# An attention stage that keeps its softmax unnormalised, sums its rows with a column of ones, and places its PSUM tiles by hand

## The chip, the cores and the metric

The program runs on one core of a Trainium2 chip. A core has TensorE (PE), VectorE (DVE), ScalarE (ACT), GpSimd (POOL), and SyncE (SP), which issues most of the DMAs. The metric is the time of one execution on the device in microseconds (us). The runs before the change took 784.77, 784.86 and 785.48 us, with a median of 784.86.

## The reference

An attention layer feeds two dense layers. Only the attention part is changed; the dense part stays as it is.

```
q, k, v: [4, 8, 576, 64]; M_prev: [4, 8, 64, 64]; z_prev: [4, 8, 64]; beta: [8]; all float32
scores = q k^T / 8, causal;   a = exp(scores - max) / (sum + 1e-9);   local = a v
phi(x) = where(x > 0, x, exp(x) - 1) + 1
mem    = (phi(q) M_prev) / (phi(q) . z_prev + 1e-6)
g      = 1 / (1 + exp(-beta))
x      = (g mem + (1 - g) local), heads side by side          -> [2304, 512]
x      = (h - tanh(h)) w_out,  h = x w_in                     (width 2048)
out    = layernorm(h softmax(h)) w_out2,  h = x w_in2         (width 1024)
```

## The kernel before

The work runs as one pass over 16 **pairs** of heads (a batch has 8 heads, so 4 pairs); then the first dense layer (class `Moe1`), then the second. The 576 queries of a head are four blocks of 128 and a tail of 64; the tails of two pairs are handled together, in the odd pair. The steps of a pair p, with lines of the kernel before:

- `load_q`, `load_k`, `load_v`: DMAs on SP. q arrives with queries on the partitions and is transposed on PE (`q_tp`, ten 64-column transposes, L224) and copied by DVE (`q_t`, L251). From pair 2 on k arrives in 32-row pieces that DVE turns itself (`k_t`, L256).
- `s_r`, `s_l`: scores on PE (L326, L342). `s_max` (L356): DVE adds the mask, moves the block from PSUM to SBUF (tile P, or PL for the tails) and takes the row's minimum of the negated scores. `s_exp` (L383): ACT, exp in place, with the row sum through `accum_out`, which is an instruction of its own in the trace (ACTIVATION_READ_ACCUMULATOR).
- `s_eps`, `s_inv` (L395, L399): DVE turns the sums into reciprocals. `s_norm` (L410): POOL multiplies each block of probabilities by the reciprocal and by 1 - g.
- `a_t` (L224): PE transposes the probabilities block by block into T; `a_ev` (L449): ACT copies T to SBUF (pt). `a_pv` (L473): PE multiplies v (the weights, 128x64) by pt, up to 256 moving columns at a time, into X.
- `f_neg` (POOL, L270), `f_exp` (ACT, L273), `f_max` (DVE, L277): phi(q) = max(q + 1, exp(min(q, 0))). `m_mm` (L291): PE, phi(q) times M and z. The weights hold both heads of the pair on 128 rows, against a block-diagonal MZ of 130 columns, into R. `m_eps`, `m_inv`, `m_mul` (L299, L303, L309): DVE divides. `a_mem` (L224): PE transposes that result into X, where `a_pv` adds to it. `x_ev` (L500): DVE copies X out; `x_mv` (L510): SP moves it by DMA into xT, the input of the dense layer.

PSUM holds three rotating "homes" of two banks (tag S) for scores, transposes and R, and a fourth (tag X) for the output of a pair alone. Order is by hand: two tables (`PROLOGUE` up to pair 7, `PERIOD` for two pairs from there) list the steps; each engine runs its instructions in the order in which they are emitted. `split_x` (L701 on ACT, L703 on POOL) splits xT by chunk of 128 channels (one pair of each batch) into a high and a low part, in `room` slots and after the pairs. `heat` (L212) is matmuls without use that keep PE running at the start. The first dense layer works on blocks n of tokens: H (L735) is h, Y (L767) is y; block 0 and 1 need only the first two batches, and twelve matmuls of H for block 0 stand among the last `a_pv`.

Of the kernel before, what the change touches and what calls it, by code (L numbers as in the profile page):

```python
# [15 lines left out]
P = 128  # L16
# [20 lines left out]

class Attention:
# [16 lines left out]
    def __init__(self, ap, sp, ps, tc, q, k, v, M_prev, z_prev, beta, xT, ident, mz):  # L55
# [44 lines left out]
        w = self.HP * 2 * self.MW  # L100
        t = mz.tile([P, 2048], F32, tag="G", name="MZ", bufs=2)
        for i in range(2):
            nc.vector.memset(t[:, w * i : w * i + w], 0.0)
            self.MZ.append(t[:, w * i : w * i + w].rearrange("p (c w) -> p c w", c=self.HP))
        self.qs = []
        for i in range(2):
            t = sp.tile([P, NC, 2, D], F32, tag=f"nq{i}", name=f"nq{i}", bufs=1)
            nc.vector.memset(t[D:P, NC - 1], 0.0)
            self.qs.append(t)
        self.poff = [P * c * (c + 1) // 2 for c in range(NC)]  # L110
        for name in ("tp", "x", "QT", "KT", "St", "e", "n", "ret", "xm", "mx", "sm", "P", "pt"):
# [19 lines left out]
    def g_inv(self, p):  # L131
# [3 lines left out]
        nc.vector.tensor_scalar(og, g, -1.0, 1.0, ALU.mult, ALU.add)  # L135

    def g_cpy(self, p):
        nc, og, D = self.nc, self.og, self.D
        pairs = og.rearrange("p (a c j) -> p c a j", c=2, j=2)
        ogL = self.ogL.rearrange("p (a j) -> p a j", j=2)  # L140
        for c in range(2):
            rows = slice(c * D, (c + 1) * D)
            nc.gpsimd.tensor_copy(ogL[rows], pairs[rows, c])

    def load_m(self, p):
# [6 lines left out]
        for j in range(2):  # L152
            rows, w = slice(j * D, (j + 1) * D), j * self.MW
            nc.sync.dma_start(
                out=t[rows, :, w : w + D],
# [3 lines left out]
                out=t[rows, :, w + D : w + D + 1],  # L159
# [3 lines left out]
    def m_gate(self, p):  # L163
# [3 lines left out]
        m = self.MZ[b % 2].rearrange("p c (j w) -> p (c j) w", w=self.MW)[:, :, 0 : self.D]  # L167
        g = self.g.unsqueeze(2).broadcast_to([P, self.H, self.D])
        self.nc.gpsimd.tensor_tensor(m, m, g, ALU.mult)

    def _natural(self, t, src, p, tail):
# [3 lines left out]
        for j in range(2):  # L175
            self.eng.dma_start(
                out=t[:, 0 : NC - 1, j],
# [3 lines left out]
            out=t[tail : tail + D, NC - 1], in_=src[b, h0 : h0 + 2, full : self.S].rearrange("h p d -> p h d")  # L181
# [6 lines left out]
    def load_k(self, p):  # L188

        D, Q = self.D, self.D // 2  # L190
        G = self.S // Q
        b, h0 = divmod(2 * p, self.H)
        t = self.sp.tile([P, P * self.NC], F32, tag="nk", name=f"k{p}", bufs=2)
        if p < self.KPE:
            t = self.nat["k", p] = t.rearrange("p (c j d) -> p c j d", j=2, d=D)
            self.nc.vector.memset(t[D:P, self.NC - 1], 0.0)
            self._natural(t, self.k, p, 0)
            return
        t = self.nat["k", p] = t[:, 0 : G * Q].rearrange("p (g d) -> p g d", d=Q)
        for j in range(2):  # L200
            for i in range(2):
# [1139 lines left out]
```

## Time and profile before

| | |
|---|---|
| median of three runs | 784.86 us |
| the profiled execution's own time | 784.9 us |
| its span, first to last instruction | 783.1 us, so 1.8 us lie around it |
| busy: PE, DVE, ACT, POOL | 768.6, 567.4, 343.8, 368.0 us |
| TensorE clock granted | 1.000 of full speed in the mean, full in all slices |

Busy time is the union of an engine's instructions. Matmuls overlap in the array, so a busy PE is not PE at its peak: for what a group of matmuls costs, take the distance from its start to the next group's start. The attention pairs fill about the first 187 us; from there to the end PE is busy without a visible gap.

### The profile page before, as it was taken

To read this page: it belongs to the slowest core of one execution; us is meant where nothing else is said; L and a number is where in the kernel's file an instruction comes from. 1 tells how busy PE (TensorE), PEld (TensorE's weight loads), DVE (VectorE), ACT (ScalarE), POOL (GpSimd) and SP (SyncE) were. 2 spreads that over 40 slices of the span, in tenths; PEclk is the share of its full clock that TensorE was granted. 3 is DMA by queue.
4 is the path that set the end of the run, shared out by engine and by line. 5 is a ranking of instruction groups with operands and counts; after the bars stand their busy time and mean duration, and the time that the engine had idled before them with its cause. 6 is when DMAs were issued, how large, how long until landed. Compare 5 with 4: busy or idle time off the path is not lost.

```text
span 783.1 us, 14732 instructions
## 1 busy us (share of the span) xinstructions
PE 768.6 (98%) x5646; PEld 648.3 (83%) x5646; DVE 567.4 (72%) x1100; ACT 343.8 (44%) x662; POOL 368.0 (47%) x352
## 2 busy tenths in 40 slices
PE   8999999999999999999999999999999999999998
PEld 6777767787888888888989889898898888888887
DVE  5999899973487786786867866677877766656651
ACT  4789999995223333332433333322422333322331
POOL 4998889976034333433433333234533444334431
PEclk9999999999999999999999999999999999999999
DMA  6665656611012221221112111112101334334341
GB/s 140 127 139 112 147 117 151 157 49 39 0 54 62 74 73 46 71 71 63 55 55 81 54 54 55 54 54 81 54 28 51 118 123 153 124 107 125 116 135 54
DMA packets 108389, 67.03 MB, mean 86 GB/s; under 512 B 85408, under 2 KB 94368, under 8 KB 108320
## 3 DMA queue, kind: packets, MB, share of 16 engines
q1 hardware_dynamic: 107120, 65.81, 30.4%
q8 instruction: 44, 0.72, 0.4%
q10 hardware_dynamic: 1200, 0.30, 0.2%
q14 instruction: 25, 0.20, 0.1%
HBM read 48.25 MB, written 13.11 MB: 78 GB/s over the span
## 4 chain that ended last, share of the span: by engine, by line
PE 87%; DVE 5%; POOL 3%; issue 2%; DMA 1%; ACT 1%; SPq 0%; DVEq 0%; ACTq 0%; POOLq 0%
PE H L735 25%; PE Y L767 25%; PE H L961 13%; PE X L473 4%; PE S L326 3%; POOL P L410 2%; DVE P L356 2%; PE R L291 2%; PE T L224 1%; DVE e L277 1%; PE heat L212 1%; PE O1X L1055 1%; PE O16X L1055 1%; PE O15S L1055 1%; PE O14X L1055 1%
## 5 line engine op out<-in xcount | busy, mean ns | idle before, releaser
L767 PE MATMUL Y<-G,wo 128*128 128x512 f32 (+1 forms) x960 | 204.4, 368 | 0.1
L767 PEld LDWEIGHTS Y<-G,wo 128*128 128x128 f32 x960 | 174.8, 188 | 24.4 <-issue 1.6
L735 PE MATMUL H<-xh,wi 128*128 128x512 f32 (+1 forms) x640 | 151.4, 369 | 0.0
L915 POOL TENSOR_TENSOR raw<-raw,cva 128x512 f32<-128x512 f32 x48 | 63.1, 1314 | 176.1 <-DVE cva L913 162.4
L735 PEld LDWEIGHTS H<-xh,wi 128*128 128x128 f32 x640 | 117.2, 188 | 16.0 <-issue 0.4
L749 ACT ACTIVATE t<-H 128x1024 f32<-128x1024 f32 (+1 forms) x40 | 37.7, 942 | 140.9 <-PE H L735 138.5
L961 PE MATMUL H<-w2i,Ys 128*128 128x512 f32 x384 | 89.6, 389 | 0.0
L410 POOL TENSOR_SCALAR P<-P,sm,og 128x512 f32<-128x512 f32 (+3 forms) x124 | 78.9, 651 | 15.2 <-DVE sm L399 8.6
L735 PE MATMUL H<-xT,wi 128*128 128x512 f32 (+1 forms) x320 | 84.6, 368 | 0.0
L961 PEld LDWEIGHTS H<-w2i,Ys 128*128 128x128 f32 x384 | 72.0, 188 | 14.9
L781 DVE TENSOR_TENSOR yT<-Y,yT 128x512 f32<-128x512 f32 (+3 forms) x105 | 77.2, 788 | 1.4 <-PE Y L767 1.2
L751 ACT CAST G<-t 128x1024 fp32r<-128x1024 f32 (+1 forms) x40 | 38.6, 965 | 84.0 <-DVE t L750 84.0
L752 DVE TENSOR_TENSOR G<-t,G 128x1024 fp32r<-128x1024 f32 (+1 forms) x40 | 45.7, 1143 | 40.4 <-ACT G L751 40.4
L383 ACT ACTIVATE P<-P,mx 128x512 f32<-128x512 f32 (+3 forms) x128 | 70.5, 556 | 2.6 <-DVE mx L356 2.5
L750 DVE TENSOR_TENSOR t<-H,t 128x1024 f32<-128x1024 f32 (+1 forms) x40 | 44.6, 1114 | 34.7 <-ACT t L749 34.6
L978 ACT ACTIVATE e<-H,s 128x1024 f32<-128x1024 f32 x18 | 20.1, 1118 | 109.6 <-DVE s L972 109.6
L735 PEld LDWEIGHTS H<-xT,wi 128*128 128x128 f32 x320 | 58.8, 188 | 7.6
L1310 POOL TENSOR_TENSOR Ys<-yT,Ys 128x512 fp32r<-128x512 f32 x16 | 20.7, 1297 | 93.2 <-ACT Ys L1309 80.4
L356 DVE CUSTOM_DVE_ANT_0 P<-S,mask 128x512 f32<-128x512 f32 (+3 forms) x128 | 56.4, 481 | 5.2 <-PE S L326 4.9
L449 ACT COPY pt<-T 128x1024 f32<-128x1024 f32 (+2 forms) x64 | 51.2, 826 | 14.5 <-PE T L224 13.6
L473 PE MATMUL X<-pt,v 128*64 128x64 f32 (+3 forms) x832 | 51.2, 272 | 0.0
L473 PEld LDWEIGHTS X<-pt,v 128*64 128x64 f32 x832 | 39.1, 137 | 12.5 <-issue 7.3
(208 smaller groups left out, 1207.9 us busy)
## 6 DMA issues: line engine op xcount, KB each, us to landing
raw<-in_moe_w_in_dram SPq DMA_DIRECT2D x24, 512.0 KB, 3.7
raw<-in_moe_w_out_dram SPq DMA_DIRECT2D x16, 512.0 KB, 3.4
D<-rest SPq DMA_DIRECT2D x16, 512.0 KB, 2.6
rest<-D SPq DMA_DIRECT2D x64, 128.0 KB, 3.0
out_dram<-ob SPq DMA_DIRECT2D x17, 256.0 KB, 3.0
nq<-in_q_dram SPq DMA_DIRECT2D x32, 128.0 KB, 2.9
v<-in_v_dram SPq DMA_DIRECT2D x32, 128.0 KB, 2.9
raw<-in_moe_w_out_dram SPq DMA_DIRECT2D x32, 128.0 KB, 2.6
```

What stands on the lines that cost most here:

```text
L356: self.nc.vector.tensor_tensor_reduce(out=self._block(p, i), in0=s, in1=mask, scale=-0.125, scalar=3.0e38, op0=ALU.add, op1=ALU.min, accum ...
L383: self.nc.scalar.activation(t, t, AF.Exp, bias=self.mx[p][:, i : i + 1], scale=-1.0, accum_out=self.sm[p][:, i : i + 1],)
L410: eng.tensor_scalar(d, d, self.sm[p][:, i : i + 1], og, ALU.mult, ALU.mult)
L449: self.copy(pt, T)
L473: self.nc.tensor.matmul(self.X[j * D : (j + 1) * D, to, D * c : D * (c + n)], v[:, kb, j, :], pt[:, r, D * at : D * (at + n)], start=False ...
L735: nc.tensor.matmul(H[a:z, f], wi[:, wl, c, f * P + a : f * P + z], self.x[n][xl][:, c], start=(count[f] == 0), stop=(count[f] == 3 * KD - ...
L750: nc.vector.tensor_tensor(t, H, t, ALU.subtract)
L752: nc.vector.tensor_tensor(G[:, 1], t, G[:, 0].bitcast(F32), ALU.subtract)
L767: nc.tensor.matmul(Y[d][:, 0:NB], wo[:, wl, f, d * P : (d + 1) * P], G[:, gl, f], start=(i == 0), stop=(i == 3 * KF - 1),)
L781: nc.vector.tensor_tensor(y, src, y, ALU.add)
L915: self.eng.tensor_tensor(w, w, a, ALU.add)
L961: nc.tensor.matmul(H[:, nh * 512 : (nh + 1) * 512], Y[:, yl, c, :], w2i[:, wl, c, nh * 512 : (nh + 1) * 512], start=(k == 0), stop=(k == 3 ...
```

## The change

- **Probabilities.** `s_exp` no longer sums, and `s_eps`, `s_inv` and `s_norm` are gone. v gets a 65th column of ones, so that PV yields the row sum as its last column.
- **PV by query.** `a_pv` swaps the operands: weights are 64 queries of pt, the moving operand is v with its ones (65 columns). 800 matmuls of 65 columns take the place of 416 of 64 to 256. The result X has queries on the partitions; `x_eps`, `x_inv`, `x_mul` (DVE) scale it by (1 - g)/sum, `x_add` (POOL) adds the memory part, `x_tp` (PE) transposes the sum, `x_ev` (now on ACT) copies it, `x_mv` moves it. `a_mem` is gone.
- **Feature map.** phi(q) = max(q, 0) + exp(min(q, 0)): `f_r` and `f_neg` on POOL, `f_exp` on ACT, `f_add` on POOL; `f_max` on DVE is gone.
- **Memory product.** `m_mm` takes one head at a time: 64 rows of weights against 65 columns of M and z, so each matmul uses a quarter of the array. 288 matmuls of 65 columns take the place of 128 of 130 and 64 of 65.
- **q.** From pair 2 on q is loaded in 32-row pieces and turned by DVE, as k is; 14 of 16 `q_tp` are gone.
- **PSUM.** All four homes are shared; the order names the home after an `@`.
- **Order.** One table for all 16 pairs replaces the two; 25 instead of 41 `heat` matmuls; all of H for block 0 and 8 of 24 matmuls of H for block 1 (`h:0`, `h:1`) stand among the last pairs.

```diff
         if tag == "S":
-            i, bufs = self.n % (3 if self.third else 2), 1
-            tag, self.n = f"S{i}", self.n + 1
-            if i == 2:
+            tag = f"S{self.homes.pop(0) if self.homes else self.n % 2}"
+            self.n, bufs = self.n + 1, 1
+            if tag == "S2":
+                tag = "X"
+            elif tag == "S3":
                 pool = self.third
...
-            t = ap.tile([P, NC, 2, D], F32, tag=f"v{i}", name=f"v{i}", bufs=1)
+            t = ap.tile([P, NC, 2, D + 1], F32, tag=f"v{i}", name=f"v{i}", bufs=1)
+            nc.gpsimd.memset(t[:, :, :, D : D + 1], 1.0)
             nc.gpsimd.memset(t[0:D, NC - 1], 0.0)
             self.vs.append(t)
...
-    def load_q(self, p):
-        t = self.nat["q", p] = self.qs[p % 2]
-        self._natural(t, self.q, p, 0)
...
+    def _load(self, name, src, p, t):
+
 
         D, Q = self.D, self.D // 2
-        G = self.S // Q
+        if p < self.KPE:
+            t = self.nat[name, p] = t.rearrange("p (c j d) -> p c j d", j=2, d=D)
+            self.nc.vector.memset(t[D:P, self.NC - 1], 0.0)
+            self._natural(t, src, p, 0)
+            return
...
+        t = self.nat[name, p] = t[:, 0 : self.S].rearrange("p (g d) -> p g d", d=Q)
         for j in range(2):
             for i in range(2):
                 at = j * D + i * Q
                 self.eng.dma_start(
                     out=t[at : at + Q],
-                    in_=self.k[b, h0 + j, :, i * Q : i * Q + Q].rearrange("(g p) d -> p g d", p=Q),
+                    in_=src[b, h0 + j, :, i * Q : i * Q + Q].rearrange("(g p) d -> p g d", p=Q),
                 )
...
+    def load_q(self, p):
+        self._load("q", self.q, p, self._next(self.qs))
+
+    def load_k(self, p):
+        self._load("k", self.k, p, self.sp.tile([P, P * self.NC], F32, tag="nk", name=f"k{p}", bufs=2))
...
+    def f_r(self, p):
+
+
+        w = self.fw[p] = self.sp.tile([P, self.S], F32, tag="fw", name=f"fw{p}", bufs=2)
+        if self.eng is self.nc.scalar:
+            self.eng.activation(w, self.QT[p], AF.Relu)
+        else:
+            self.eng.tensor_scalar_max(w, self.QT[p], 0.0)
+
     def f_neg(self, p):
-        e = self.e[p] = self.sp.tile([P, self.S], F32, tag="fe", name=f"e{p}", bufs=3)
-        self.eng.tensor_scalar_min(e, self.QT[p], 0.0)
+        e = self.e[p] = self.sp.tile([P, self.S], F32, tag="fe", name=f"e{p}", bufs=4)
+        self.nc.gpsimd.tensor_scalar_min(e, self.QT[p], 0.0)
...
-    def f_max(self, p):
+    def f_add(self, p):
         e = self.e[p]
-        self.nc.vector.scalar_tensor_tensor(e, self.QT[p], 1.0, e, ALU.add, ALU.max)
-        self.scores -= 1
+        self.nc.gpsimd.tensor_tensor(e, e, self.fw.pop(p), ALU.add)
...
     def m_mm(self, p):
...
-        for i in range(self.NC):
-            at = min(P * i, self.S - P)
-            for j, n in ((0, 1), (1, 1)) if i == self.NC // 2 else ((0, 2),):
-                r, u = divmod(2 * i + j, self.NC)
+        for i in range(n + p % 2):
+            for j in range(2):
                 for h in range(2):
+                    rows, q = slice(j * D, (j + 1) * D), p - 1 + h if i == n else p
+                    at = self.full if i == n else P * i + D * h
                     self.nc.tensor.matmul(
-                        R[h * D : (h + 1) * D, r, W * u : W * (u + n)], f[:, at + h * D : at + h * D + D],
-                        self.MZ[b % 2][:, c, W * j : W * (j + n)], start=True, stop=True, skip_group_check=True,
+                        R[h * D : (h + 1) * D, j, W * i : W * (i + 1)], self.e[q][rows, at : at + D],
+                        self.MZ[b % 2][rows, q % self.HP], start=True, stop=True, skip_group_check=True,
                     )
-        self.ret[p] = R[:, :, 0 : W * self.NC].rearrange("p r (u w) -> p r u w", w=W)
...
+    def _times(self, p, tag, t, n):
+
+        w = 2 * n.shape[2] * self.D
+        x = self.ap.tile([P, P * self.NC], F32, tag=tag, name=f"{tag}{p}", bufs=2)[:, 0:w]
+        n = n.unsqueeze(3).broadcast_to([*n.shape, self.D])
+        self.nc.vector.tensor_tensor(
+            x.rearrange("p (u r d) -> p r u d", r=2, d=self.D), t[:, :, :, 0 : self.D], n, ALU.mult
+        )
+        return x
...
     def m_eps(self, p):
-        n = self.n[p] = self.ap.tile([P, 2, self.NC], F32, tag="fn", name=f"n{p}")
+        n = self.n["m", p] = self._n(p)
         self.nc.vector.tensor_scalar_add(n, self.ret[p][:, :, :, self.D], 1e-6)
...
     def m_mul(self, p):
-        D = self.D
-        x = self.xm[p] = self.ap.tile([P, self.NC, P], F32, tag="xm", name=f"xm{p}", bufs=2)
-        n = self.n.pop(p).unsqueeze(3).broadcast_to([P, 2, self.NC, D])
-        self.nc.vector.tensor_tensor(
-            x.rearrange("p c (j d) -> p (c j) d", j=2).rearrange("p (r u) d -> p r u d", r=2),
-            self.ret.pop(p)[:, :, :, 0:D], n, ALU.mult
+        self.xm["m", p] = self._times(p, "xm", self.ret.pop(p), self.n.pop(("m", p)))
+
+    def x_eps(self, p):
+        n = self.n["x", p] = self._n(p)
+        GI = self.GI[:, p % self.HP, :, 0 : n.shape[2]]
+        self.nc.vector.scalar_tensor_tensor(n, self._units(self.X[p], p)[:, :, :, self.D], 1e-9, GI, ALU.add, ALU.mult)
+
+    def x_inv(self, p):
+        n = self.n["x", p]
+        self.nc.vector.reciprocal(n, n)
+
+    def x_mul(self, p):
+        self.xm["x", p] = self._times(p, "xa", self._units(self.X.pop(p), p), self.n.pop(("x", p)))
+
+    def x_add(self, p):
+        x, m = self.xm["x", p], self.xm.pop(("m", p))
+        self.eng.tensor_tensor(x, x, m, ALU.add)
+
+    def x_tp(self, p):
+        x = self.xm.pop(("x", p))
+        T = self.tp["x", p] = self._home(f"XT{p}")
+        self._turn(T, [x[:, P * c : P * (c + 1)] for c in range(self.NC - 1 + p % 2)])
+
+    def x_ev(self, p):
+        n = self.NC - 1 + p % 2
+        x = self.x[p] = self._next(self.xs)[:, 0 : P * n]
+        self.copy(
+            x.rearrange("p (n r w) -> p r n w", r=2, w=self.D), self._order(self.tp.pop(("x", p)), n)
         )
...
-            accum_out=self.sm[p][:, i : i + 1],
...
-    def s_norm(self, p, i):
-        d = self.P[p, "b", i]
...
-        eng = self.nc.vector if p == self.NP - 1 and i % 2 else self.nc.gpsimd
-        eng.tensor_scalar(
-            d, d, self.sm[p][:, i : i + 1], og, ALU.mult, ALU.mult
-        )
...
     GROUPS = [
-        [(j, 0, c) for j in range(2) for c in range(4)],
-        [(j, kb, c) for j in range(2) for kb, c in ((1, 1), (1, 2), (1, 3), (3, 3))],
-        [(j, 2, c) for j in range(2) for c in (2, 3)],
+        [(j, kb, 3) for j in range(2) for kb in range(4)],
+        [(j, kb, 2) for j in range(2) for kb in range(3)],
+        [(j, kb, c) for c in (1, 0) for j in range(2) for kb in range(c + 1)],
     ]
-
-    def a_mem(self, p):
-
-        x = self.xm.pop(p)
-        self.X = self._home(f"X{p}", "X")
-        self._turn(self.X, [x[:, c] for c in range(self.NC)], keep=True)
...
-    PV = [
-        [(0, 0, 4, 0)],
-        [(1, 1, 3, 0), (3, 3, 1, 3)],
-        [(2, 2, 2, 0)],
-    ]
...
     def a_pv(self, p, i):
 
-        D = self.D
-        v = self.vs[p % 3]
+
+        D, W, n = self.D, self.MW, self.NC - 1
+        if p not in self.X:
+            self.X[p] = self._home(f"X{p}")
+        X = self.X[p]
         if i < 3:
             todo = [
-                (kb, j, self.pt[p, i], r, at + j * len(self.GROUPS[i]) // 2, n, r, c)
-                for kb, c, n, at in self.PV[i] for r in range(2) for j in range(2)
+                (self.pt[p, i], at, self.vt[p], kb, j, r, c)
+                for at, (j, kb, c) in enumerate(self.GROUPS[i]) for r in range(2)
             ]
         else:
             todo = [
-                (kb, j, self.pt[p - p % 2, 3 + j], p % 2, kb, 1, 1, self.NC - 1)
-                for kb in range(self.NC) for j in range(2)
+                (self.pt[p, 3 + j], kb, self.vt[p - 1 + r], kb, j, r, n)
+                for j in range(2) for kb in range(n + 1) for r in range(2)
             ]
-        for kb, j, pt, r, at, n, to, c in todo:
+        for pt, at, v, kb, j, r, c in todo:
             self.nc.tensor.matmul(
-                self.X[j * D : (j + 1) * D, to, D * c : D * (c + n)],
-                v[:, kb, j, :],
-                pt[:, r, D * at : D * (at + n)],
-                start=False, stop=False, skip_group_check=True,
+                X[r * D : (r + 1) * D, j, W * c : W * (c + 1)],
+                pt[:, r, D * at : D * (at + 1)],
+                v[:, kb, j],
+                start=kb == 0, stop=kb == c, skip_group_check=True,
             )
...
-    def x_ev(self, p):
-        x = self.x[p] = self.ap.tile([P, P * self.NC], F32, tag="x", name=f"x{p}", bufs=2)
-        self.copy(
-            x.rearrange("p (c r w) -> p r c w", r=2, w=self.D), self._order(self.X, self.NC)
-        )
...
+    ORDER = """
+        load_q:0:s load_k:0:a heat:0:-:17@1 k_tp:0:-@0 load_q:1:s q_tp:0:-@1 k_t:0:a load_k:1:s
...
+        f_add:14:- h:0:-@2 a_ev:14:a:2 a_ev:14:a:0 x_tp:12:-@3 x_ev:12:a s_exp:15:-:1 s_max:15:-:7
...
+        for op in self.ORDER.split():
+            op, _, homes = op.partition("@")
+            name, i, engine, *part = op.split(":")
+            self.ps.homes = [int(h) for h in homes]
+            part = [int(x) for x in part]
...
-        def filler():
-            rooms.finish()
-            for n in range(2):
-                H = ps.tile([P, m.KF, 512], F32, tag="S", name=f"H0_{n}", bufs=2)
-                yield from m.h_step(0, n, H, per=4)
-
-        fill = filler()
-        some = islice(fill, 11)
+        def filler(n):
+            H = ps.tile([P, m.KF, 512], F32, tag="S", name=f"H0_{n}")
```

On PE, in the middle of the pass: the memory product R of one pair, and PV (X) of another, before. Weights come behind the arrow with the moving tile; the sizes are those of the output.

```order
L326 MATMUL S_2_1987<-kT_1782,qT_1887 128x384 x2
L473 MATMUL X_1936<-pt_2_1893,v_113 64x128 x4
L291 MATMUL R_2008<-MZ,e_1747 64x130 x4
L291 MATMUL R_2008<-MZ,e_1747 64x65 x4
L291 MATMUL R_2008<-MZ,e_1747 64x130 x4
L473 MATMUL X_1936<-pt_3_1812,v_113 64x64
L473 MATMUL X_1936<-pt_4_1804,v_113 64x64
```

The same place after the change, for pairs of the same parity.

```order
L408 MATMUL S_1_2339<-kT_2156,qT_2192 128x128 x2
L241 MATMUL XT_2344<-ident,xa_2073 128x64 x10
L322 MATMUL R_2368<-MZ,e_1766 64x65 x16
L514 MATMUL X_2388<-v_111,pt_0_2358 64x65 x16
L514 MATMUL X_2388<-v_111,pt_2_2276 64x65 x12
L514 MATMUL X_2388<-v_111,pt_1_2305 64x65 x12
L514 MATMUL X_2388<-v_117,pt_3_2162 64x65
L514 MATMUL X_2388<-v_111,pt_3_2162 64x65
```

R is now 16 (odd pairs 20) matmuls of 65 columns, PV 40 (odd pairs 60) of 65, and the transpose XT of the finished output stands ahead of the next pair's work.

On ACT, at the end of the attention pass, before: the last copies of transposed probabilities (pt), and the first casts of `split_x` for block 3 of the tokens (xh_3647; its chunk c needs pair 12 + c).

```order
L449 COPY pt_3_3409<-T_3_3393 128x640
L701 CAST xh_3647<-xT_84 128x384 x2
L449 COPY pt_2_3465<-T_2_3452 128x512
L449 COPY pt_1_3516<-T_1_3469 128x1024
L449 COPY pt_0_3518<-T_0_3499 128x1024
L701 CAST xh_3388<-xT_84 128x512 x4
L701 CAST xh_3647<-xT_84 128x384
L749 ACTIVATE t_0_3589<-H_0_3523 128x1024
```

After: xs<-XT_3714 and xs<-XT_3779 are `x_ev` of pairs 14 and 15, xh_3852 is block 3.

```order
L493 COPY pt_0_3618<-T_0_3582 128x1024
L380 COPY xs<-XT_3600 128x2x5x64
L961 CAST wo_124<-raw 128x512
L380 COPY xs<-XT_3714 128x2x4x64
L737 CAST xh_2635<-xT_83 128x512
L737 CAST xh_3852<-xT_84 128x384 x3
L380 COPY xs<-XT_3779 128x2x5x64
L785 ACTIVATE t_0_3803<-H_0_3410 128x1024
L789 CAST G_0_3802<-t_0_3803 128x1024
```

Three casts of block 3 (chunks of pairs 12, 13, 14) now stand ahead of `x_ev` of pair 15; before, two stood ahead of the last pair's copies. POOL has the same: the three subtractions of block 3 stand ahead of `x_add` of pair 15 (xa_3711).

```order
L739 TENSOR_TENSOR xT_83<-xT_83,xh_2635 128x512
L739 TENSOR_TENSOR xT_84<-xT_84,xh_3852 128x384 x3
L370 TENSOR_TENSOR xa_3711<-xa_3711,xm_3762 128x640
L739 TENSOR_TENSOR xT_84<-xT_84,xh_3753 128x512 x4
L739 TENSOR_TENSOR xT_84<-xT_84,xh_3852 128x384
```

And PE between the transposes of pair 14 (XT_3714) and pair 15 (XT_3779):

```order
L241 MATMUL XT_3714<-ident,xa_3541 128x64 x8
L771 MATMUL H_0_3410<-xh_1830,wi_123 128x512 x4
L322 MATMUL R_3728<-MZ,e_3213 64x65 x16
L322 MATMUL R_3728<-MZ,e_3096 64x65
...
L771 MATMUL H_0_3410<-xT_83,wi_123 128x512 x4
L771 MATMUL H_1_3770<-xh_2635,wi_123 128x512 x8
L241 MATMUL XT_3779<-ident,xa_3711 128x64 x10
L771 MATMUL H_1_3770<-xT_83,wi_123 128x512 x4
L771 MATMUL H_1_3770<-xh_2635,wi_123 128x512 x8
```

Sixteen matmuls of H and the 20 of R (the last four are single rows, of which one is shown) stand between the two; the other 16 of H for block 1 come behind XT of pair 15.

## Rows read from the trace of the kernel before

**Rows 1.** Page, parts 1 and 2: busy us (share) xinstructions; clock in 40 slices.

```profile
PE 768.6 (98%) x5646; PEld 648.3 (83%) x5646; DVE 567.4 (72%) x1100; ACT 343.8 (44%) x662; POOL 368.0 (47%) x352
PEclk9999999999999999999999999999999999999999
```

**Rows 2.** First 180 us: busy PE, PEld, DVE, ACT, POOL; clock; DMA share; GB/s.

```profile
0.00:180.00 180.00, 169.05 (x2766) 131.22 (x2768) 157.46 (x497) 153.20 (x390) 150.29 (x194) 1.00 0.57 125
```

**Rows 3.** PE's timeline, 160 to 215 us: start, us, line, tile, shape, records.

```profile
166.54 0.66 PE L473 MATMUL X<-pt,v 128*64 128x128 f32 x8
167.03 1.29 PE L291 MATMUL R<-MZ,e 128*64 128x130 f32 x24
168.15 2.50 PE L473 MATMUL X<-pt,v 128*64 128x64 f32 x44
170.58 1.52 PE L224 MATMUL T<-ident,P 64*128 64x64 f32 x40
171.94 0.48 PE L224 MATMUL X<-ident,xm 64*128 64x64 f32 x10
172.34 0.66 PE L473 MATMUL X<-pt,v 128*64 128x128 f32 x8
172.93 0.83 PE L224 MATMUL T<-ident,PL 64*128 64x64 f32 x20
...
189.67 1.98 PE L735 MATMUL H<-xh,wi 128*128 128x512 f32 x8
...
195.11 11.04 PE L767 MATMUL Y<-G,wo 128*128 128x512 f32 x48
```

**Rows 4.** PE's timeline, 99 to 122 us: groups of short matmuls.

```profile
100.21 0.29 PE L342 MATMUL S_L<-kT,qT 64*64 64x64 f32 x8
...
105.80 0.40 PE L291 MATMUL R<-MZ,e 128*64 128x65 f32 x8
...
116.45 0.47 PE L224 MATMUL N11q<-ident,nq 64*128 64x64 f32 x10
116.85 1.34 PE L291 MATMUL R<-MZ,e 128*64 128x130 f32 x24
```

**Rows 5.** Who PE waited for up to 187 us: total, times, longest.

```profile
PE T L224 <- DVE mx L356: 3.1, 5, 0.8
PE S L326 <- DVE mx L356: 1.6, 5, 0.4
```

**Rows 6.** ACT's groups up to 195 us: busy us, mean ns.

```profile
L383 ACT ACTIVATION_READ_ACCUMULATOR P<-P,mx 128x1 f32 x128 | 24.6, 192 | 0.0
...
L701 ACT CAST xh<-xT 128x384 fp32r<-128x384 f32 x8 | 3.7, 519 | 0.0
...
L251 ACT COPY kT<-N0k 128x640 f32<-128x640 f32 x1 | 0.7, 693 | 4.7 <-PE N0k L224 4.7
```

**Rows 7.** POOL's groups: busy us, mean ns.

```profile
L410 POOL TENSOR_SCALAR P<-P,sm,og 128x512 f32<-128x512 f32 (+3 forms) x124 | 78.9, 651 | 15.2 <-DVE sm L399 8.6 <-ACT pt L449 3.8 <-PE S L326 2.2
L270 POOL TENSOR_SCALAR e<-qT 128x576 f32<-128x576 f32 x16 | 29.1, 1818 | 5.4 <-DVE qT L251 5.3
...
L410 POOL TENSOR_SCALAR PL<-PL,sm,ogL 128x576 f32<-128x576 f32 x15 | 12.4, 826 | 2.0 <-ACT P L383 1.7
L915 POOL TENSOR_TENSOR raw<-raw,cva 128x512 f32<-128x512 f32 x4 | 5.2, 1299 | 0.0
```

**Rows 8.** DVE's groups up to 187 us: busy us, mean ns.

```profile
L277 DVE SCALAR_TENSOR_TENSOR e<-qT,e 128x576 f32<-128x576 f32 x16 | 18.3, 1146 | 0.0
L500 DVE COPY x<-X 128x640 f32<-128x640 f32 x16 | 13.1, 821 | 10.7 <-PE X L473 10.6
L309 DVE TENSOR_TENSOR xm<-R,n 128x640 f32<-128x640 f32 x16 | 13.0, 814 | 0.1
...
L395 DVE TENSOR_SCALAR sm<-sm 128x6 f32<-128x6 f32 (+2 forms) x32 | 9.7, 321 | 2.2 <-ACT P L383 2.2
```

**Rows 9.** DMA issues up to 185 us: times, KB each, median us to landing.

```profile
xT<-x SPq DMA_DIRECT2D x11, 256.0 KB, 2.4
```

More of the change, by code (lines that the diff above doesn't have):

```diff
@@ L23, in __init__ @@
     def __init__(self, pool):
-        self.pool, self.n, self.third = pool, 0, None
+        self.pool, self.n, self.homes = pool, 0, []
     def tile(self, shape, dtype, tag, name, bufs=1):
@@ L135, in g_inv @@
         nc.vector.tensor_scalar(og, g, -1.0, 1.0, ALU.mult, ALU.add)
+        nc.vector.reciprocal(og, og)
     def g_cpy(self, p):
[L138 to L143, printed above, removed]
+        D, GI, n = self.D, self.GI, self.NC - 1
+        g, og = (t.rearrange("p (c j) -> p c j", j=2) for t in (self.g, self.og))
+        for i in range(2):
+            rows = slice(i * D, (i + 1) * D)
+            self.eng.tensor_copy(self.gm[rows], g[rows, :, i])
+        for r in range(2):
+            self.eng.tensor_copy(GI[:, :, r, 0:n], og[:, :, r].unsqueeze(2).broadcast_to([P, self.HP, n]))
+        for i in range(2):
+            rows = slice(i * D, (i + 1) * D)
+            self.eng.tensor_copy(GI[rows, 1::2, :, n], og[rows, i::2])
     def load_m(self, p):
@@ L152, in load_m @@
         for j in range(2):
-            rows, w = slice(j * D, (j + 1) * D), j * self.MW
+            rows = slice(j * D, (j + 1) * D)
             nc.sync.dma_start(
-                out=t[rows, :, w : w + D],
+                out=t[rows, :, 0:D],
                 in_=self.M[b].rearrange("(c j) d e -> j d c e", j=2)[j],
@@ L158, in load_m @@
             nc.sync.dma_start(
-                out=t[rows, :, w + D : w + D + 1],
+                out=t[rows, :, D : D + 1],
                 in_=self.z[b].rearrange("(c j) (d o) -> j d c o", j=2, o=1)[j],
@@ new lines, in m_mm, with _n @@
+        if p % 2:
+            del self.e[p - 1], self.e[p]
+        self.ret[p] = self._units(R, p)
+        self.scores -= 1
+    def _n(self, p):
+        t = self.ap.tile([P, 2, self.NC], F32, tag="xn", name=f"n{p}", bufs=4)
+        return t[:, :, 0 : self.NC - 1 + p % 2]
+    def _times(self, p, tag, t, n):
[6 more added lines that the diff above has]
+        return x
@@ new lines, in x_ev, with x_mv @@
+    def x_ev(self, p):
[3 more added lines that the diff above has]
+            x.rearrange("p (n r w) -> p r n w", r=2, w=self.D), self._order(self.tp.pop(("x", p)), n)
+        )
+    def x_mv(self, p):
+        b, c = divmod(p, self.HP)
+        x, full, S = self.x.pop(p), self.full, self.S
+        for xt, t0, a, e in self.xT(b * S, b * S + full):
+            self.nc.sync.dma_start(out=xt[:, c, t0 : t0 + e].bitcast(F32), in_=x[:, a : a + e])
+        if p % 2:
+            tails = x[:, full:].rearrange("p (i w) -> p i w", i=2)
+            for xt, t0, a, e in self.xT(b * S + full, (b + 1) * S):
+                self.nc.sync.dma_start(
+                    out=xt[:, c - 1 : c + 1, t0 : t0 + e].bitcast(F32), in_=tails[:, :, a : a + e]
+                )
+        self.done.add(p)
@@ L333, in s_l @@
         nc, D, S, full = self.nc, self.D, self.S, self.full
-        t = [self.ps.tile([P, 1024], F32, tag="S", name=f"S{p}_L{j}", bufs=2) for j in range(2)]
+        t = [self.ps.tile([P, 1024], F32, tag="S", name=f"S{p}_L{j}") for j in range(2)]
         for j in range(2):
@@ L351, in s_max @@
         if p not in self.mx:
[L352 to L355 removed]
+            self.mx[p] = self.ap.tile([P, self.LAST + 2], F32, tag="mx", name=f"mx{p}")
         self.nc.vector.tensor_tensor_reduce(
@@ L612, in run @@
+    """
+    def run(self, fills):
+        nc = self.nc
         on = {
@@ L622, in emit @@
             getattr(self, name)(i, *part)
[L624 to L650 removed]
+        for op in self.ORDER.split():
[3 more added lines that the diff above has]
+            part = [int(x) for x in part]
+            if name == "room":
+                self.room(int(i), *part)
+            elif name == "h":
+                next(fills[int(i)], None)
+            else:
+                emit(name, int(i), engine, part)
+            yield
 class Moe1:
@@ L1158, in attention_moe_kernel @@
             drain.finish()
-            for _ in fill:
-                pass
+            for f in fills:
+                for _ in f:
+                    pass
     ps.third = None
```

330 lines of the change are left out of this document (154 added, 176 removed).

## The prediction

> **What bounds the kernel now.** I read the page first. PE is busy for 98% of the span and its clock is granted in full throughout [rows 1]; the reader is to see that no clock can be won or lost, and that in the dense layers, where nothing is changed, time is PE's alone. So what the attention stage gains or loses comes through in full. Next came the busy time of the first 180 us, which hold nearly all of the stage [rows 2]: PE 169.1, DVE 157.5, ACT 153.2, POOL 150.3. All four are 83 to 94% busy, so one engine made lighter would gain little by itself: the next would hold the stage.
>
> Then I read PE's timeline for what a group costs, from its start to the next one's [rows 3]. R (`m_mm`) takes 167.03 to 168.15, 1.12 us. PV of a pair is a group of 8 (0.49) and one of 44 (168.15 to 170.58, 2.43), 2.92 together. `a_mem` takes 0.40 (171.94 to 172.34), and so does a `q_tp` (116.45 to 116.85) [rows 4]. R comes once a pair: from 116.85 to 167.03 are five pairs, 10.0 us each [rows 3, 4]. PE's waits are short and mostly for DVE to free a PSUM home (`s_max`), 3.1 and 1.6 us in all [rows 5]. PE is therefore nearly closed up, and the forecast is made on PE, with a check that no other engine comes in its way.
>
> **The price of a 65-column matmul.** PV's, R's and S_L's matmuls use half or a quarter of the array, and several run at once. Two groups of 8 records give the price [rows 4]: R's last 8, on column halves, run two at a time, four positions, and take 0.40; S_L's last 8, on quarters, run four at a time, two positions, and take 0.29. With a latency l and a step s for each further position, l + 3s = 0.40 and l + s = 0.29, so s = 0.055 and l = 0.235. A position costs 0.055 us whether it holds two matmuls or four. Each matmul of the program is two records here (832 of PV for 416).
>
> **PE, part by part.**
> - PV: 800 matmuls, 50 a pair, 100 records on column halves, 50 positions: 2.75 us, against 2.92 now. The 65 columns may cost a little more than in R's few, so I take no change; the bound is -0.17 a pair, -2.7 in all.
> - R: 288 matmuls, 18 a pair, 36 records on quarters, 9 positions: 0.50 against 1.12. That is -0.62 a pair, -9.9 in all. If they ran only two at a time, 18 positions would cost 0.99, and the gain is 2.1 in all. I take the quarters, since S_L shows them.
> - `q_tp`: 14 fall away, 14 x 0.40 = -5.6.
> - `a_mem` of ten transposes becomes `x_tp` of nine on average: 16 x 0.04 = -0.6.
> - Fewer `heat` matmuls, at the start, where PE waits for data: nothing; what covers it is that wait, and without it the 16 matmuls would be a further gain.
> - Switches between ways of dividing the array: a group of 8 takes 0.49 when R, divided alike, follows, and 0.59 (172.34 to 172.93) when a transpose, divided otherwise, follows [rows 3]: 0.10 a switch. The Trainium skill, "TensorEngine Tiling (Array Packing)", Key Properties, says that changing the tiling mode, not just the tile, drains TensorE; the trace agrees. It speaks against this change, since R leaves the division that it shared with PV. Counted along PE's order up to the first Y there are 85 switches before and 90 after: +0.5. Without any price for them the sum would be 0.5 lower.
>
> Together -15.6. PE will not turn all of it into time, since it will reach some probabilities sooner than they are ready: I take nine tenths, -14.0.
>
> **The other engines, so that none takes PE's place.** ACT loses the sums, 24.6 us, and 16 of the same kind for the tails at 0.19 (3.1), and gains `x_ev` at 0.69 (the copy of 640 from PSUM) or less, at most 11.1 [rows 6]: 153.2 becomes 136.6. POOL loses `s_norm`, 78.9 + 12.4; it gains `f_r`, priced as `f_neg` at 29.1 in all, and two adds a pair of 576 elements on average; the nearest row has 1.30 for two inputs of 512, so 1.46 each, 46.8 in all [rows 7]: 150.3 becomes 134.9. DVE loses `f_max` (18.3), `x_ev` (13.1) and `s_eps` (9.7), and gains `x_mul` as `m_mul` (13.0) with `x_eps` and `x_inv` at no more than `s_eps` cost a piece (32 x 0.32 = 10.3) [rows 8]: 157.5 becomes at most 139.7; q's transposes take the place of copies of the same number. Each engine thus falls by some 15 to 18, as PE does, and the balance stays as it is. In place of an `s_norm` that held back transposes, POOL's `f_r`, `f_neg` and `f_add` now hold back R, and `x_add` the XT; both have a pair or more of other work ahead of them.
>
> **The end of the stage.** Here the order adds a wait. `x_tp` of pair 15 waits for `x_add`, and on POOL this stands behind three subtractions of block 3, the last of which needs pair 14 in xT. From the end of XT of pair 14: `x_ev` 0.69, the DMA 2.4 [rows 9], a cast of 384 at 0.52 [rows 6], the subtraction 0.97 (1.30 for 512, by columns), `x_add` of 640 at 1.62 (by columns) [rows 7]: 6.2. PE has 16 matmuls of H at 0.227 (24 records from 189.67 to 195.11 [rows 3]), 3.6, R at 0.55 for pair 15 and four switches: 4.6. It waits for the other 1.6, and behind XT stand the rest of H and all of Y. On ACT, `x_ev` of pair 15 stands behind the same chunk's cast, and the tanh of H behind it. I take +2; bounds 0 (the DMA lands early) and 6.2 (nothing covers it).
>
> **Sum.** -14.0 + 2 = -12. The profiled execution took 784.9 us (span 783.1 and 1.8 around it), as the median of the runs, 784.86: 773.
>
> **Rivals.**
> - *R does not run four at a time.* For: the quarters of S_L belong to one group of 64 columns, and R changes weights with every matmul. Against: so does S_L. Cost 7.8 of the gain: 780. By the Trainium skill, "TensorE: Matmul & The Clock Gate", section "Wait — 56ns, not 53.3ns?", start-to-start never drops below about 25 ns: R's 576 records would then take 14.4 us in place of 8.0, and the time would be 779. The rows of S_L disagree: 8 records within 0.055 and a latency.
> - *The waits go too.* Four shared homes and a lighter DVE take away PE's 4.7 us of waits for `s_max` [rows 5], all of the -15.6 arrives, and the end costs nothing: 784.9 - 15.6 - 4.7 = 764.6.
> - *The gain stays in the waits.* PE reaches each probability sooner, but the chain scores, exp, transpose, copy keeps its length, and the pairs follow one another every 10.0 us as before: 784 to 786, no change.
> - *Slower: `x_ev` on ACT.* It stands in ACT's order among exps and copies, which wait behind it, and PE behind these. It needs `x_add` on POOL, behind `f_neg` and `f_r` at 1.8 each. For: ACT is in the cycle now. Against: the order puts `x_ev` a pair or more behind its PV. If it is late by 0.75 us a pair, the gain is gone; at 1.0 us, 16 us more: 789.
>
> **Chances and range.** The forecast 0.57 (its own range 768 to 778), R in twos 0.10, the waits go 0.20, no change 0.07, slower 0.06. The range takes in the second and third with their bounds and leaves the last two out: 764 to 782. A change of 0.2% is 1.6 us, about what a measurement of this kernel can tell from none: faster 0.87, same 0.07, slower 0.06.
>
> **What would show it.** In the profile after: R's group of 32 or 40 records takes about 0.5 us to the next start; PV's 80 to 120 records some 55 ns a position; R follows R every 9.1 to 9.3 us; POOL, ACT and DVE each lose 15 us or more up to the end of the stage; PE waits 1 to 3 us ahead of XT of pair 15; Y starts 11 to 14 us earlier than at 195.1. The prediction is wrong if R is paced in twos, if PE's waits for POOL or ACT grow by more than 0.3 us a pair, or if the dense layers change in length.

## The result, and the profile after

The changed kernel takes 778.5 us (median of 8 runs, 775.0 to 782.5), the kernel before 785.2 in the same rounds: a ratio of 0.9915, 95% interval 0.9888 to 0.9941. It is faster by just under one per cent, and the time lies within the range, but of the 12.1 us that were forecast 6.7 arrived. The profiled execution is the best of the eight: 775.0, span 773.2, so 9.9 under its counterpart of before.

Windows after, to be held against [rows 2] (columns as there), the second ending where Y starts:

```profile
0.00:180.00 180.00, 165.27 (x3622) 133.75 (x3624) 126.51 (x444) 148.42 (x263) 127.28 (x111) 1.00 0.62 127
0.00:184.71 184.71, 169.44 (x3642) 136.86 (x3642) 127.76 (x446) 151.14 (x267) 127.28 (x111) 1.00 0.61 125
```

The same window of before, up to its first Y:

```profile
0.00:195.11 195.11, 184.16 (x2870) 142.73 (x2871) 161.10 (x500) 160.73 (x403) 160.00 (x203) 1.00 0.53 118
```

Y starts 10.4 us earlier; what follows takes 588.5 in place of 588.0. So the whole difference lies in the attention stage. PE's busy time up to Y fell by 14.7, and its idle time rose from 10.9 to 15.3. PE's timeline after shows both (start, us, then as in [rows 3]; what PE waited for in brackets):

```profile
98.64 0.81 PE L322 MATMUL R<-MZ,e 64*64 64x65 f32 x40
99.38 2.55 PE L514 MATMUL X<-v,pt 128*64 128x65 f32 x80
104.01 0.53 PE L241 MATMUL T<-ident,PL 64*128 64x64 f32 x10 [2.08 <-DVE mx L435]
105.09 0.92 PE L408 MATMUL S<-kT,qT 64*128 64x384 f32 x4 [0.56 <-DVE n L359]
...
110.31 0.69 PE L322 MATMUL R<-MZ,e 64*64 64x65 f32 x32
110.93 3.14 PE L514 MATMUL X<-v,pt 128*64 128x65 f32 x100
115.63 0.80 PE L514 MATMUL X<-v,pt 128*64 128x65 f32 x20 [1.56 <-issue]
...
160.66 2.55 PE L514 MATMUL X<-v,pt 128*64 128x65 f32 x80
163.15 0.53 PE L241 MATMUL T<-ident,PL 64*128 64x64 f32 x10
...
168.18 3.72 PE L514 MATMUL X<-v,pt 128*64 128x65 f32 x120
171.83 0.46 PE L241 MATMUL XT<-ident,xa 64*128 64x64 f32 x8
...
175.14 2.01 PE L771 MATMUL H<-xh,wi 128*128 128x512 f32 x8
179.80 0.53 PE L241 MATMUL XT<-ident,xa 64*128 64x64 f32 x10 [2.65 <-POOL xa L370]
```

R takes 0.74 (98.64 to 99.38) or 0.62, on average 0.68 where [rows 3] had 1.12. PV takes 2.49 or 3.65, on average 3.07 against 2.92. And PE stands still at three places that [rows 5] do not have: 2.08 at 102, 1.56 at 114 and 2.65 at 177. The last was forecast. The second has no cause that the profile names ("issue": PE waited for nothing that it shows), and it is not k's: end_mz, a run below in which k is in time, has it at the same matmuls (its timeline):

```profile
111.69 0.81 PE L514 MATMUL X<-v,pt 128*64 128x65 f32 x21 [1.59 <-issue]
```

The first begins at a wait that the kernel before had nowhere, DVE's for k (the waits, 20 to 185 us: total, times, longest):

```profile
DVE kT L274 <- DMA k<-in_k_dram: 11.7, 7, 3.9
```

DVE stops in its order at the transpose of k (3.9 us, up to 100.7), and the masked scores behind it, which PE needs out of their PSUM homes, come late. SP, which issues that k, shows why (SP's timeline; here the time is that of issuing):

```profile
93.73 2.16 SPq L209 DMA_DIRECT2D nq<-in_q_dram  x4
95.94 3.01 SPq L209 DMA_DIRECT2D k<-in_k_dram  x4
99.05 2.47 SPq L388 DMA_DIRECT2D xT<-xs  x4
```

Each row starts where the one ahead ended. From 49.6 to 146.0 the rows of SP add up to 91.5 of 96.4 us, short waits within a row counted in; in the kernel before, the same stretch adds up to 79.7, with four gaps of 2 to 4 us. q now takes four issues a pair in place of three, and the pairs come faster.

### The profile page after: what moved, and what is told of

Its sections match the earlier page's. It is cut to its first block, busy times and chain, and to the rows that moved or that the text cites. A ratio compares the mean times of both kernels' runs of the same rounds, so it can differ in the third digit from the quotient of the medians.

```text
span 773.2 us, 16000 instructions
## 1 busy us (share of the span) xinstructions
PE 754.5 (98%) x6418; PEld 642.4 (83%) x6418; DVE 535.3 (69%) x1046; ACT 338.0 (44%) x534; POOL 344.7 (45%) x268
## 4 chain that ended last, share of the span: by engine, by line
PE 86%; ACT 4%; DMA 3%; DVE 3%; SPq 2%; POOL 1%; issue 1%; DVEq 0%; ACTq 0%; POOLq 0%
PE Y L806 25%; PE H L771 25%; PE H L1000 13%; PE X L514 4%; PE S L408 3%; PE T L241 2%; DMA k<-in_k_dram 1%; SPq L209 1%; ACT pt L493 1%; DVE P L435 1%; PE S_L L424 1%; PE R L322 1%; ACT P L462 1%; DMA xT<-xs 1%; PE O1X L1094 1%
## 5 line engine op out<-in xcount | busy, mean ns | idle before, releaser
L462 ACT ACTIVATE P<-P,mx 128x512 f32<-128x512 f32 (+3 forms) x128 | 67.0, 564 | 0.6 <-DVE mx L435 0.6
L493 ACT COPY pt<-T 128x768 f32<-128x768 f32 (+2 forms) x64 | 51.0, 827 | 9.6 <-PE T L241 9.4
L514 PE MATMUL X<-v,pt 128*64 128x65 f32 x1600 | 51.2, 223 | 2.2 <-issue 2.1
L514 PEld LDWEIGHTS X<-v,pt 128*64 128x64 f32 x1600 | 48.4, 138 | 4.7 <-issue 3.2
L408 PE MATMUL S<-kT,qT 64*128 64x256 f32 (+3 forms) x256 | 44.1, 454 | 2.0 <-DVE n L359 1.7
```

The lines of the kernel that those rows point to most:

```text
L408: nc.tensor.matmul(s, Q[rows, P * r : P * r + P], K[rows, 0:w], start=True, stop=True, skip_group_check=True,)
L462: self.nc.scalar.activation(t, t, AF.Exp, bias=self.mx[p][:, i : i + 1], scale=-1.0,)
L493: self.copy(pt, T)
L514: self.nc.tensor.matmul(X[r * D : (r + 1) * D, j, W * c : W * (c + 1)], pt[:, r, D * at : D * (at + 1)], v[:, kb, j], start=kb == 0, stop= ...
```

## Where the other half went: a control

The profiled execution was at full clock; the listed runs were not. Their mean granted clock goes from 1.000 (775.0) down to 0.989 (782.5), while before's runs read 0.999 or 1.000.

**again** is the changed kernel unedited.

> The changed kernel once more, with nothing edited, as the measure of the three others. If the spread of its times (775.0 to 782.5) goes with the granted clock, as the listed means of 1.000 to 0.989 suggest, this run's profile may hold a stretch where the clock is under full, and the windows show where. Expected 775 to 782 by both theories.

It took 779.6 (779.1 to 781.3). One of its windows, and under it the same one of the first profile, which had full clock:

```profile
140.00:160.00 20.00, 16.95 (x394) 13.35 (x392) 13.01 (x49) 16.30 (x31) 15.45 (x12) 0.91 0.47 130
```

```profile
140.00:160.00 20.00, 19.17 (x480) 15.74 (x477) 14.72 (x55) 19.45 (x37) 16.18 (x12) 1.00 0.47 133
```

A mean of 0.91 over 20 us is some 3.6 us at 1.2 in place of 2.4 GHz; from 100 to 120 us it is 0.91 as well, behind a wait of 1.95. PE's timeline of this run puts the one shown behind a wait too:

```profile
141.29 2.64 PE L514 MATMUL X<-v,pt 128*64 128x65 f32 x80
146.43 0.52 PE L241 MATMUL T<-ident,PL 64*128 64x64 f32 x10 [2.50 <-DVE mx L435]
147.51 1.15 PE L408 MATMUL S<-kT,qT 64*128 64x384 f32 x4 [0.56 <-DVE n L359]
...
149.23 2.20 PE L424 MATMUL S_L<-kT,qT 64*64 64x512 f32 x16
151.36 1.13 PE L241 MATMUL T<-ident,P 64*128 64x64 f32 x28
```

S_L's 16 records take 2.13 to the next start; in the first profile, which kept its clock, they take 1.14 there (146.36 to 147.50). The chain of waits names what came late: 

```profile
138.78 4.26 DMA k<-in_k_dram
```

At 62 us both executions are level. From there to Y again needs 3.9 us more:

```profile
62.10:188.70 126.60, 115.36 (x2618) 93.26 (x2616) 84.81 (x289) 105.32 (x185) 87.47 (x63) 0.97 0.54 120
```

```profile
62.00:184.71 122.71, 112.57 (x2618) 91.91 (x2616) 83.60 (x290) 105.03 (x185) 87.26 (x63) 1.00 0.55 123
```

2.8 of them are PE's busy time, the same matmuls at a mean clock of 0.97; 1.1 are idle time.

## The experiments

Two theories stood against each other. *SP's issues set the pace*: the loads are late because their queue never stops. *Slow transfers*: they are late because q's and k's 128-byte pieces take long (this k 4.3 us, the median 2.7). All times below are medians of 4 to 6 runs, next to before at 784.9 to 785.6.

**mv_act**: in `x_mv`, `nc.sync.dma_start` becomes `nc.scalar.dma_start`.

> Only x_mv (the transfers of the finished output into xT) is issued from ACT's queue in place of SP's. Theory 'queue': between 50 and 146 us SP issues without a gap, and k and v arrive late because of it (DVE waits 11.7 us for k); x_mv is 27 of SP's 134 us. Then k is no longer waited for, PE's idle time between 22 and 175 us (9.0) falls by 2 to 4, and the median falls by 2 to 5 us, or by less if ACT, which then issues, becomes late. Rival 'transfer': k is late because the 16 DMA engines are busy with 128-byte pieces (share 0.62); then the same bytes take as long from either queue, DVE's waits for k stay, and the time stays within 1 us or rises.

787.7, and DVE waited for k as long as in again (15.5 and 13.3). But SP got a wait of its own (SP's waits, 20 to 180 us):

```profile
SPq L209 <- DMA xT<-xs: 14.2, 5, 4.6
```

By its letter this is the rival's outcome (k is waited for as before, the time rises). But SP's loads stood waiting for transfers of the other queue, so SP was not freed, and the run tells nothing of either theory.

**mv_pool**: the same with `nc.gpsimd.dma_start`.

> x_mv issued by POOL in place of SP. From ACT's queue it made SP wait 14 us for the transfers into xT, so that run told nothing of the theories. If POOL's queue does not hold SP back, theory 'SP's issues set the pace' expects SP's stretch of 27 us to be free for loads, k in time and 772 to 777; the rival 'slow transfers' 778 or more. If POOL takes over 1 us for an issue, f_r, f_neg and f_add behind it come late and the time rises above 780 whatever the cause.

772.7 (768.9 to 776.5): 6.9 under again, as the theory of the issues expects. DVE's waits for k fall, of the same bytes in the same pieces:

```profile
DVE kT L274 <- DMA k<-in_k_dram: 3.5, 3, 1.8
```

**more_issues** and **fewer_issues** change the number of issues and hardly anything else; the second leaves out part of the loads, as its expectation says.

```diff
-        self.eng.dma_start(
-            out=t[tail : tail + D, NC - 1, :, 0:D], in_=src[b, h0 : h0 + 2, full : self.S].rearrange("h p d -> p h d")
-        )
+        for j in range(2):
+            self.eng.dma_start(out=t[tail : tail + D, NC - 1, j, 0:D], in_=src[b, h0 + j, full : self.S])
```

> The tail of v in two transfers in place of one: one more issue on SP a pair, the same bytes in the same pieces. Theory 'SP's issues set the pace': SP issues back to back between 50 and 146 us at 0.5 to 0.6 us each, so some ten more of them put every load behind by up to 6 us; k and v come later, PE waits more, the time rises by 2 to 6 us against the changed kernel (779). Rival 'the transfers themselves are slow' (the k that is waited for takes 4.3 us to land): an issue more of a small transfer changes nothing, 779 within 1.5.

> Left out: the loads of v's last 64 rows from pair 4 on and of z from the third batch on (what stands there already is used in their place), 16 of SP's issues, some 10 us of its time, and under 3% of the bytes. Theory 'SP's issues set the pace': k and v are in time, DVE's waits for k (12 to 13 us) halve at least, PE's waits of about 2 us behind them go, and with them the clock's two drops of 3.4 us; 772 to 776. Rival 'slow transfers': k is waited for as before, 778 to 780.

788.0 and 772.3: 8.4 over and 7.3 under again. DVE's waits for k, first with more, then with fewer:

```profile
DVE kT L273 <- DMA k<-in_k_dram: 16.1, 5, 8.2
```

```profile
DVE kT L276 <- DMA k<-in_k_dram: 4.9, 4, 2.8
```

The second is as the theory expects: sixteen issues fewer give 7.3. The first goes beyond its 2 to 6, and its trace says less for the theory than its time does. The line that it changes also loads q and k of the first two pairs, so 20 issues are added, four of them at the start. Up to Y the profiled execution is 8.9 behind again's, and 5.9 of these are there at R of pair 1 (in again at 41.85):

```profile
22.70 1.24 PE L321 MATMUL R<-MZ,e 64*64 64x65 f32 x32 [1.80 <-POOL MZ L180]
...
47.73 0.81 PE L321 MATMUL R<-MZ,e 64*64 64x65 f32 x40
```

There R waits for M, and the clock is at its lower level from 23 to 36 us. So it is the runs that take issues off SP that show what SP costs. That a slow transfer adds to a single wait (4.3 us in again) is not excluded; it is not what decides.

**end_dve**: `x_add:15:p` becomes `x_add:15:v`, `x_ev:15:a` becomes `x_ev:15:v`. **mz**: in `load_m`, the four `nc.sync.dma_start` of a batch become `nc.gpsimd.dma_start`. **end_mz**: both.

> x_add and x_ev of pair 15 on DVE in place of POOL and ACT, so that neither stands behind the subtraction and the cast of block 3. The step 'end of the stage' of the prediction: PE's wait of 2.65 us ahead of XT of pair 15 goes, Y starts 2 to 3 us earlier, and the time falls by 2 to 3 us. Rival: something else ends last there (the transfer of pair 14 into xT, the casts of H); then the wait reappears behind XT and the time stays within 0.7 us.

> The changed kernel with only the loads of M and z issued by POOL; pair 15 as in the change. With end_dve and end_mz it completes a square of two edits: 779.6 with neither, 776.4 with the end's edit, 766.6 with both. If the two are independent: 769 to 771, with the wait of 2 to 3 us ahead of XT of pair 15 still there and the clock whole up to there. Rival: the gain of end_mz over end_dve needed the end's edit (its wait too lets the clock fall); then 772 to 776.

> As end_dve (x_add and x_ev of pair 15 on DVE), and the loads of M and z issued by POOL, 16 issues less on SP with nothing left out. Theory 'SP's issues set the pace': 1 to 4 us under end_dve's 776.4, most of it around 100 us, where four such issues (2.6 us) stand ahead of the k that is waited for. Rival: within 1 us of end_dve.

776.4, 770.1 and 766.6, against 779.6 with neither: -3.2, -9.5 and -13.0, so the two add up; for end_mz only 1 to 4 under end_dve had been expected. mz leaves nothing out and moves the same bytes. Its waits for k, and the loads of k in again and in mz (60 to 180 us: issues, KB each, median us to landing):

```profile
DVE kT L274 <- DMA k<-in_k_dram: 1.0, 3, 0.5
```

```profile
k<-in_k_dram SPq DMA_DIRECT2D x33, 72.0 KB, 2.7
```

```profile
k<-in_k_dram SPq DMA_DIRECT2D x28, 72.0 KB, 3.0
```

A k takes no less time to land and is in time all the same, since SP comes to it earlier. SP's issues set the pace of the changed kernel.

In end_mz all four runs (766.1 to 767.7) show full clock; its ratio to before is 0.9765 (0.9752 to 0.9777), the best version here. PE up to its first Y, at 176.73:

```profile
0.00:176.73 176.73, 168.07 (x3643) 136.20 (x3643) 133.18 (x448) 150.36 (x266) 137.21 (x126) 1.00 0.64 131
```

PE is busy 1.4 less than in the first profile and idles 8.7 in place of 15.3. In mz the wait at the end is still there, and the clock falls behind it:

```profile
174.33 0.52 PE L241 MATMUL XT<-ident,xa 64*128 64x64 f32 x10 [2.82 <-POOL xa L370]
174.78 1.53 PE L771 MATMUL H<-xT,wi 128*128 128x512 f32 x4
176.11 3.28 PE L771 MATMUL H<-xh,wi 128*128 128x512 f32 x8
```

Eight H's that take 3.11 here to the next start (to 179.22) take 1.82 in end_mz (174.00 to 175.82). Removing that wait is worth 3.5 here: the wait, and some of the clock.

**before_mz**: mz's edit in the kernel before.

> The kernel before, with nothing but the loads of M and z issued by POOL. Theory 'the change made SP the bound': before, pairs came every 10 us, SP had gaps and DVE waited for no k, so freeing SP of 10 us changes nothing: within 1.5 us of 785. Rival 'SP bound both kernels': 3 us or more faster, and then the change itself is worth less than its own trace says.

793.5, 8.6 slower: both expectations fell. POOL did more than I had seen: four issues cost it 2.6 us, and behind them stood `s_norm`. PE's waits in before_mz:

```profile
PE T L224 <- POOL P L410: 7.6, 10, 1.1
```

The kernel before has, in the same stretch (20 to 195 us):

```profile
PE T L224 <- POOL P L410: 1.3, 2, 0.8
```

These 6.3 are most of the 8.6; the clock fell in this run too (0.993 to 0.998). So the run cannot say whether SP held the kernel before; that it did not rests on the trace alone, in which DVE waits for no k and SP has its gaps. The change took `s_norm` from POOL, and there the same edit gains 9.5.

**end_mz_mv**: end_mz with `x_mv` on POOL as well.

> end_mz with x_mv issued by POOL as well, 43 of SP's issues in all moved away. If SP still holds the loads back in end_mz (PE idles 6.9 us up to Y there), 763 to 766; if what is left is PE's own work and waits for DVE and ACT, within 1 us of 766.6, or more by what POOL's issues cost f_r and x_add.

771.0, 4.4 over end_mz. DVE's waits for k are down to 0.4, so SP is no longer short. PE has a new wait of 3.3 for ACT's copy pt, and ACT waited 2.9 just ahead of it for POOL (raw). From 61 us to Y POOL is busy, issues included, for 108.5 of 118.4 us, in end_mz for 92.6 of 115.4: by this trace POOL now issues too much.

**heat41** and **end_mz_heat**: four entries of the order raised by four each, 25 heat matmuls to 41 (`heat:0:-:1@0` to `heat:0:-:5@0`, and so on).

> 41 heat matmuls in place of 25, as many as before the change, 16 more in four places between 12 and 27 us. Theory 'clock': the changed kernel's clock falls in some executions because PE does less in the start; then the clock is 1.000 in all runs, the times lie within 1 us of each other at 775 to 777. Rival: the clock falls for another reason or elsewhere; then the spread of 7 us stays, and the time rises by 0 to 3 us for the 16 matmuls.

> end_mz with 41 heat matmuls in place of 25, now without late loads behind them. The prediction put the removed heat matmuls at nothing, since PE waits for data there. If so, within 0.7 us of 766.6. If they stand on the path, 2 to 4 us more (16 at some 0.2 each are 3.2), which the change then had gained.

784.2 and 770.2: 4.6 over again and 3.6 over end_mz. The 16 matmuls stand on the path. The clock fell in heat41 as well (0.989 to 0.993), behind later waits, so they do not keep it up. At the start they may: four profiles with 25 (mv_act, mv_pool, more_issues, fewer_issues) show the lower level at some time between 22 and 36 us, behind waits of 1.8 to 2.7 us, and the two with 41 do not; but six others with 25 do not either. From fewer_issues:

```profile
28.00:32.00 4.00, 4.00 (x50) 2.80 (x49) 1.10 (x3) 1.74 (x4) 0.48 (x1) 0.50 0.67 109
```

## Why the prediction was right in sign and range, and 5.5 us short

- **What binds.** Right: the gain is PE's work (-14.7 against -15.6, though the heat matmuls are in the first and not in the second), and the dense layers did not move.
- **R**: the quarters run four at a time, which the rival denied: 32 records (two to a matmul) in 0.62 are 19 ns each, below the 25 ns of the Trainium skill's "TensorE: Matmul & The Clock Gate" (section "Wait — 56ns, not 53.3ns?"). The step was nearly right too: ten positions take 0.74 and eight 0.62, 0.06 for each further one, where 0.055 was taken. What the sum left out is a fixed part of every group: 0.62 less eight steps of 0.058 is 0.16. It counts once a group (a change of division, 0.10 in the prediction, lies in it), and the prediction gave R none, though its own l + 8s is 0.675. So nine positions cost 0.68, not 0.50: -0.44 a pair, -7.0 in place of -9.9.
- **PV**: forty positions take 2.49 and sixty 3.65, so 0.058 a position and again 0.16. Fifty are 3.07: +2.4 where nothing was taken, outside my bound.
- **`q_tp`, `a_mem`**: the groups of `q_tp` are gone; but in the kernel before they took from 0.31 (131.13 to 131.44) to 0.58 (109.21 to 109.79) to the next start, so -5.6 is rough. XT takes 0.24 to 0.40.
- **Heat at nothing**: wrong. I called PE's wait for data the cover. The runs price the 16 matmuls at 3.6, which the change had gained. R and PV at +5.3 and heat at -3.6 cancel in great part, and that is luck.
- **Switches**: +0.5, not measured by itself.
- **Nine tenths**: the size (1.6) was right for the profiled execution (4.3 more idle time, 2.65 of it at the end), the reason was not. PE is not early for its probabilities: k is late, and 1.56 has no cause that the profile names.
- **The other engines**: this is the step that failed. Over the first 180 us DVE fell by 31.0 and POOL by 23.0, more than the 17.8 and 15.4 worked out. ACT fell by 4.8, not 16.6: I added up the sums' rows whole, and rows of ACT overlap. In the kernel before, exp and sum together take 0.38 from 97.34 to 97.72:

```profile
97.34 0.39 ACT L383 ACTIVATE P<-P,mx 128x128 f32<-128x128 f32 x1
97.63 0.19 ACT L383 ACTIVATION_READ_ACCUMULATOR P<-P,mx 128x1 f32 x1
97.72 0.39 ACT L383 ACTIVATE P<-P,mx 128x128 f32<-128x128 f32 x1
```

  After, an exp alone goes from 98.18 to 98.48, 0.30. Wherever the next instruction follows at once, the medians to its start are 0.385 and 0.294 at 128 columns, 0.706 and 0.613 at 512: a sum costs some 0.09, and 144 of them 13, not 27.7. That cost no time here. What cost time is that the list had no SP: "the balance stays as it is" left out the queue that issues the loads. Its waits for `x` looked like slack, and q's fourth issue a pair was not counted. Taking the 16 issues of M and z off it gives back 9.5 (mz). The Trainium skill, "Perfetto Trace Analysis", section "What 'DMA-bound' means", names an issuing engine whose track is solid with DMA instructions as a bound of its own; SP from 50 to 146 us, with 91.5 of 96.4, is that case.
- **The end of the stage**: +2, measured 2.65, and end_dve gives back 3.2.
- **No clock can be lost**: true of the kernel before, and taken over for the one after without reason. In again and in mz, waits of 2.5 and 2.8 us on PE are followed by the lower level, and seven of the eight runs have a mean clock under full; in again the clock is 2.8 of the 3.9 that it loses against the profiled execution. end_mz has neither wait and full clock in all its runs. But such a wait is not enough, since the profiled execution kept its clock through 2.08 and 2.65, and not needed: in the profile of end_mz_heat the clock falls behind 1.12 and 0.56.

```profile
142.55 0.52 PE L241 MATMUL T<-ident,PL 64*128 64x64 f32 x10 [1.12 <-DVE mx L435]
143.63 0.93 PE L408 MATMUL S<-kT,qT 64*128 64x384 f32 x4 [0.56 <-DVE n L359]
...
145.13 2.20 PE L424 MATMUL S_L<-kT,qT 64*64 64x512 f32 x16
```

  What decides stays open.
- **No change** and **slower by `x_ev`**: from 61.9 to 98.6 us R follows R every 8.8 to 9.6, 9.2 in the mean as forecast, until k is late, and PE waits for ACT no longer than 0.5 at a time.
- **The waits go too** (764.6, a chance of 0.20): not what the change did. With SP freed and the end repaired it takes 766.6, near that number and by another sum: R and PV cost more than in it, heat gives more.
- **Number and signs**: of the 5.5, 2.0 are in the profiled execution (775.0), whose Y comes 10.4 and not 12 earlier; the other 3.5 lie between it and the median, where again's trace has more work at the lower clock (2.8) and more idle time (1.1). So 778.5 is 0.5 above the forecast's own range of 768 to 778. Two signs that were named fail: Y was to start 11 to 14 earlier, and ACT was to lose 15 up to it and loses 9.6.

## What to carry to other kernels

When a change shortens the pair on the binding engine, divide each queue's issuing time by the new period as well: a queue that fills 83% of a stretch before has little left for loads that come 9% faster and one issue more. Price a group as a fixed part and a step, from two long rows of one kind and from start to next start. And a wait on PE may cost more than its length, as the clock can fall behind it; look at the granted clock of several runs, not of the profiled one alone.

## What the runs showed of the hardware

Groups of fp32 matmuls of 65 columns cost 0.058 us a position and 0.16 a group, whether a position holds two halves of the array (PV) or four quarters (R). An issue from POOL of a load of M or z took about as long as one from SP (0.6 to 0.7 us each), and takes POOL's own time. `x_mv` on ACT's queue made SP's loads wait 14.2 us for transfers into xT. With the clock at its lower level S_L's group took 2.13 in place of 1.14 and eight H's 3.11 in place of 1.82; it came behind waits of 1.1 to 2.8 us on PE, and not behind all of these.
